# Backward kernel of a speech joint on one core: the last chunk's eight u taken together, with two u on the partitions

## The chip, the cores and the metric

The kernel runs on one core of a Trainium2 chip. The metric is the device time of one execution in microseconds; lower is better. TensorE (PE) multiplies and turns tiles, VectorE (DVE) and ScalarE (ACT) work element by element and empty PSUM, GpSimd (POOL) does small copies and issues a few DMAs, and SyncE (SP) issues nearly all DMAs.

## The reference, cut to what matters

Two strided convolutions with a gelu turn x into f (one row for four rows of x); f and g are mapped by w_f and w_g, added for every pair of a row t and one of eight u, sent through tanh and mapped by w_o. The kernel returns that output and the gradients of all seven inputs.

```python
B, T, D, K = 2, 16000, 256, 3
U = 8
def _fwd_reference(x, w1, w2, g, w_f, w_g, w_o):
    ...
    h = _gelu(h)[:, ::2, :]          # after a convolution of x with w1
    ...
    f = _gelu(f)[:, ::2, :]          # after a convolution of h with w2
    fe = jnp.einsum("btd,de->bte", f, w_f)
    ge = jnp.einsum("bud,de->bue", g, w_g)
    j = jnp.tanh(fe[:, :, None, :] + ge[:, None, :, :])
    return jnp.einsum("btud,dv->btuv", j, w_o)

def reference(x, w1, w2, g, w_f, w_g, w_o, grad_out):
    _out, _vjp = jax.vjp(_f, x, w1, w2, g, w_f, w_g, w_o)
    _grads = _vjp(grad_out)
    return (_out0, *[jnp.asarray(_g) for _g in _grads])
```

All data are bf16; grad_out is [2, 4000, 8, 256].

## The kernel before

The 8000 rows of f (2 batches of 4000) are cut into 17 chunks: one of 256 rows (two blocks of 128), fifteen of 512 (four blocks of 128), and a last one of 64 rows (one block of 64). A chunk g_ goes through three stages:

- `stage_a`: the two convolutions, gelu and its derivative, FE = f by w_f (channels on the partitions), and from the third chunk on `fe_rows`, which turns FE into rows (FER). HR, the rows of h and f, come by a DMA transpose.
- `stage_j`: for each of four pairs of u, `pair(up)` computes JT = tanh(FE + GE) on ACT (L670); JR, the same in rows, from FER + GEB on DVE (L694) and a tanh on ACT (L699); GWO, the gradient of w_o, as JR by GO, the rows of grad_out (one long accumulation in a PSUM bank of its own); for each u the product of GOT (grad_out transposed by DMA) with WOT (w_o turned), which the DVE step L739 multiplies with JSQ - 1 into NGZ while it sums it into NGP (for the gradient of g); the sum over u in ZS, and at the last u in GN (L754); and the output JT by WO, emptied into OUT and stored.
- `stage_de`: from GN back through w_f, w2 and w1: GN (L862), GH (L881, L902), each with a one-column shift (`halo`, on POOL), their rows GNR and GHR (DMA transposes, in the last chunk `pe_rows` on PE, L787), the weight gradients (`wgrad`), and GX, the gradient of x. The w1 gradient of the two last chunks is made at the end by `last_w1`, whose i = 0 part reuses the bank of GWO.

In the last chunk a pair has 64 rows: its GWO matmuls have 64 rows, its output matmuls 64 columns of weights, its GOT matmuls 64 columns of data.

The instructions' order is not written by hand. `op` puts every operation on a list with its engine, an estimated cost, its dependences and a priority (`at`, else `F.now`; in units of rows of f, 512 for a chunk, so one unit is about 0.1 us). `Flow.issue` plays these through with the estimated costs (`c_pe`, `c_act`, `c_dve`, the landing time `land` of a DMA) and gives out, one after another, the operation that could start first, at equal start the one with the lowest priority value. So each engine's order is fixed when the kernel is built. Buffers come in classes with a fixed number of slots (go 4, got 3, jt 3, jr 3, out 3, hr 2, ghr 1, gnr 1, PSUM 7); an operation that opens a buffer waits until a slot is free, and buffers of a class are opened in the order in which they were asked for.

At the start ACT issues the loads of w1 (three), w_f and w_g, with a small gelu between, which brings ACT's table in; POOL issues the loads of g and w_o; SP issues x, w2 and the rest. `turn` transposes weights on PE; w_o's turn gives WOT and has the priority of the middle of chunk 0's convolutions.

Of the kernel before, what the change touches and what calls it, by code (L numbers as in the profile page):

```python
# [188 lines left out]
def c_pe(ns):  # L189
    return sum(max(n / 2.4 + 2.5, 25.0) for n in ns)  # L190
# [20 lines left out]
def kernel(  # L211
# [329 lines left out]
    def stage_a(g_, t0, dt):  # L541
# [60 lines left out]
        if g_ >= NTR:  # L602
            fe_rows(g_)
# [20 lines left out]
    n_gwo = sum(c.nb for c in chunks) * U * KT  # L624
# [29 lines left out]
    def stage_j(g_, t0, dt):  # L654
# [7 lines left out]
        def pair(up):  # L662
# [13 lines left out]
            for h in range(max(nb // 2, 1)):  # L676
# [33 lines left out]
                gwo_ops.append(op("PE", c_pe([V] * (4 * na)), gwo, r=[JR, GO], w=[], at=tu + q * (h / 2 + 0.3)))  # L710
            OUT = buf("out", [P, NB, 2, V], BF16, "OUT_SB")
            for step in range(4):
# [44 lines left out]
                if step < nb:  # L757
                    a = step
                    ps = psum()

                    def out_mm(e, a=a, ps=ps):
                        for jj in range(2):
                            for kt in range(KT):
                                mm(ps[:n_, jj * V:(jj + 1) * V], JT[:, jj, kt, a * n_:(a + 1) * n_], WO[:, kt, :],
                                   kt == 0, kt == KT - 1)
                    op("PE", c_pe([V] * 4), out_mm, r=[JT, WO, (OUT, "b")], w=[ps], new=[ps] + ([OUT] if a == 0 else []))
                    evac(lambda a=a: OUT[:n_, a].rearrange("p u v -> p (u v)"), lambda ps=ps: ps[:n_, :], 512,
                         r=[ps], w=[(OUT, a)])
# [9 lines left out]

    def pe_rows(g_, name, cls, SRC, lo, nblk, m):
        R = buf(cls, [P, 2 * NB + (cls == "ghr"), D], BF16, name)  # L780
# [8 lines left out]
        op("PE", c_pe([P] * (nblk * KT)), trs, r=[SRC, ident], w=[ps], new=[ps, R])  # L789
# [3 lines left out]
    def grad_rows(g_, name, cls, SRC, nblk, m):  # L793
        if chunks[g_].last:
            return pe_rows(g_, name, cls, SRC, 1, nblk, m)
        return tile_rows(g_, name, cls, SRC, nblk, lo=1, shape=[P, 2 * NB + (cls == "ghr"), D],
                         land=3000.0 if g_ == LAST - 1 else 8000.0)
# [265 lines left out]
    def gwg_out():  # L1063
# [10 lines left out]
    CONVS = 4  # L1074
    GEBX = 1.2
# [5 lines left out]
       r=[(warm, 0)], w=[(warm, 1)])  # L1081
# [17 lines left out]
    wload("ACT", WG, 0, lambda: WG[:], lambda: w_g.rearrange("(kt p) n -> p kt n", p=P), BIG, 7000.0)  # L1099
# [5 lines left out]
    wload("POOL", WO, 0, lambda: WO[:], lambda: w_o.rearrange("(kt p) n -> p kt n", p=P), BIG + 2, 9000.0)  # L1105
# [51 lines left out]
    for k in range(NG + 1):  # L1157
        c = chunks[min(k, LAST)]
        t0, Wk = float(c.q0 if k < NG else NQ), float(c.W) if k < NG else 300.0
        if k < NG:  # L1160
            if k in (NTR, CB, CB + 1):
                load_geb(c, lambda up, t0=t0, Wk=Wk, k=k: t0 + Wk * (up / UP - (GEBX if k == NTR else 0.5)))
            for up in range(UP):
# [4 lines left out]
        if k < NG:  # L1168
            stage_j(k, t0, Wk)
# [49 lines left out]
```

## Time and profile before

| what | value |
|---|---|
| median of 3 runs | 782.3 us (781.51 to 782.38) |
| the profiled execution | 781.06 us, span 779.0 us |
| PE busy | 767.7 us (99% of the span), 5641 matmuls |
| DVE, ACT, POOL busy | 718.2, 710.5, 84.0 us |
| granted PE clock | 0.999 |
| last matmul starts / span ends | about 774 / 779.0 us |
| DMA | 183.82 MB, mean 236 GB/s |

Durations in the profile come from the profiled execution; the span is counted from its first to its last record, and the execution's own time is 2.06 us more. A group of matmuls is shown from the first start to the last end; matmuls overlap, so two groups' starts tell more than their busy times. Most matmuls have line 315, the helper `mm`, so they are told apart by their tiles.

### The profile page before, as it was taken

The numbers are of one execution on the slowest core, as the hardware profiler recorded it, in microseconds if no ns is written. First come the engines' busy times: TensorE is split into PE (matmuls) and PEld (weight loads), VectorE is DVE, ScalarE is ACT, GpSimd is POOL, SyncE is SP. The second block draws the span as 40 slices with busy tenths as digits, with TensorE's granted clock in tenths as the row PEclk, the third lists the DMA queues.
The fourth block names the chain that finished last, engine by engine and source line by source line (L and its number), as shares of the span: only waits on it lengthen the run. The fifth ranks groups of instructions, "written<-read, shape, count | busy, mean of one in ns | idle before, by whom it ended". The sixth has DMA issues, their size and how long they took to land.

```text
span 779.0 us, 15414 instructions
## 1 busy us (share of the span) xinstructions
PE 767.7 (99%) x5641; PEld 533.0 (68%) x5641; DVE 718.2 (92%) x1511; ACT 710.5 (91%) x1145; POOL 84.0 (11%) x223
## 2 busy tenths in 40 slices
PE   8999999999999999999999999999999999999997
PEld 6765767576676766767577675766767667677765
DVE  4989999998999999999999999989999899999874
ACT  5989999999999999999999999899999999999752
POOL 2001010101102010020110202001020010201000
PEclk9999999999999999999999999999999999999999
DMA  9999999999999999999999999999999999989783
GB/s 182 228 250 230 230 232 265 250 228 273 205 252 241 240 293 223 280 236 238 257 252 283 204 249 252 236 283 212 272 238 223 254 223 291 191 225 244 187 177 109
DMA packets 393624, 183.82 MB, mean 236 GB/s; under 512 B 318145, under 2 KB 386668, under 8 KB 391628
## 3 DMA queue, kind: packets, MB, share of 16 engines
q1 hardware_dynamic: 391226, 181.64, 102.5%
q10 hardware_dynamic: 2178, 1.05, 0.5%
q8 instruction: 44, 0.72, 0.4%
q0 software_dynamic: 144, 0.15, 0.2%
q14 instruction: 32, 0.26, 0.1%
HBM read 52.99 MB, written 50.35 MB: 133 GB/s over the span
## 4 chain that ended last, share of the span: by engine, by line
PE 89%; ACT 6%; DVE 3%; DMA 2%; issue 1%; ACTq 0%
PE ps L315 74%; PE GWO L315 14%; ACT JT L670 2%; DMA WG<-in_w_g_dram 1%; PE psb L616 1%; ACT JSQ L730 1%; ACT HT L499 1%; ACT g_sq L497 1%; DMA W<-in_w_dram 0%; DVE NGZ L739 0%; ACT JR L699 0%; ACT OUT_SB L324 0%; DVE g_s L501 0%; DVE ZS L754 0%; ACT g_s L509 0%
## 5 line engine op out<-in xcount | busy, mean ns | idle before, releaser
L670 ACT ACTIVATE JT<-FE,GE 128x512 bf16<-128x512 bf16 (+4 forms) x288 | 178.9, 683 | 0.0
L739 DVE SCALAR_TENSOR_TENSOR NGZ<-JSQ,ps 128x512 f32<-128x512 bf16 (+3 forms) x252 | 150.8, 607 | 2.1 <-PE ps L315 1.9
L315 PE MATMUL ps<-WO,JT 128*128 128x256 bf16 (+1 forms) x1008 | 150.5, 273 | 0.3 <-DVE NGZ L739 0.2
L315 PE MATMUL ps<-GOT,WOT 128*128 128x512 bf16 (+2 forms) x544 | 149.9, 362 | 0.3 <-DVE g_s L501 0.3
L730 ACT ACTIVATE JSQ<-JT 128x1024 bf16<-128x1024 bf16 (+2 forms) x129 | 131.0, 1015 | 11.1 <-DVE NGZ L739 8.3
L315 PEld LDWEIGHTS <-JT 128*128 128x128 bf16 (+1 forms) x1008 | 98.3, 98 | 58.3 <-issue 0.4
L324 ACT CAST OUT_SB<-ps 128x512 bf16<-128x512 f32 (+1 forms) x205 | 121.7, 605 | 14.8 <-PE ps L315 14.3
L699 ACT ACTIVATE JR<-JR 128x1024 bf16<-128x1024 bf16 (+1 forms) x116 | 123.5, 1066 | 9.6 <-DVE JR L694 9.6
L315 PE MATMUL GWO<-GO_R,JR 128*128 128x256 bf16 (+1 forms) x1008 | 130.8, 273 | 0.6 <-DVE JR L329 0.6
L754 DVE TENSOR_TENSOR ZS<-ZS,NGZ 128x1024 f32<-128x1024 f32 (+2 forms) x102 | 115.3, 1130 | 0.7
L315 PEld LDWEIGHTS <-JR 128*128 128x128 bf16 (+1 forms) x1008 | 98.2, 98 | 15.8 <-DVE JR L329 0.9
L315 PEld LDWEIGHTS <-W 128*128 128x128 bf16 x636 | 60.0, 98 | 59.8 <-issue 0.7
L315 PE MATMUL ps<-W1T,GH 128*128 128x256 bf16 (+2 forms) x506 | 94.6, 325 | 1.3 <-ACT FE L324 1.2
L315 PE MATMUL ps<-XC,W 128*128 128x512 bf16 (+2 forms) x432 | 86.5, 351 | 0.1
L315 PE MATMUL ps<-GHR,XR 128*128 128x256 bf16 (+1 forms) x736 | 83.3, 273 | 0.0
L315 PEld LDWEIGHTS <-XR 128*128 128x128 bf16 (+1 forms) x756 | 73.7, 98 | 8.6
L694 DVE TENSOR_TENSOR JR<-FER,GEB 128x1024 bf16<-128x1024 bf16 (+1 forms) x116 | 78.0, 673 | 0.0
L315 PEld LDWEIGHTS <-WOT 128*128 128x128 bf16 x544 | 51.0, 98 | 29.6 <-issue 1.9
L819 DVE TENSOR_TENSOR ACC<-ACC,ps 128x512 f32<-128x512 f32 x87 | 57.4, 679 | 14.4 <-PE ps L315 14.3
L315 PEld LDWEIGHTS <-GH 128*128 128x128 bf16 (+1 forms) x506 | 49.4, 98 | 26.3 <-issue 1.9
L326 ACT ACTIVATE GX_SB<-ps 128x512 bf16<-128x512 f32 (+1 forms) x89 | 52.0, 608 | 13.8 <-PE ps L315 13.5
L497 ACT ACTIVATE g_sq<-ps 128x512 bf16<-128x512 f32 (+2 forms) x102 | 57.6, 565 | 2.8 <-PE ps L315 2.8
(131 smaller groups left out, 984.2 us busy)
## 6 DMA issues: line engine op xcount, KB each, us to landing
GO_R<-in_grad_out_dram SPq DMA_DIRECT2D x60, 512.0 KB, 5.2
out_dram<-OUT_SB SPq DMA_DIRECT2D x60, 512.0 KB, 5.5
XR<-in_x_dram SPq DMA_DIRECT2D x15, 1088.0 KB, 8.6
out_dram<-GX_SB SPq DMA_DIRECT2D x30, 512.0 KB, 3.3
GOT<-GO_R SPq DMA_TRANSPOSE x68, 5.3
GO_R<-in_grad_out_dram SPq DMA_DIRECT2D x4, 256.0 KB, 4.1
out_dram<-OUT_SB SPq DMA_DIRECT2D x4, 256.0 KB, 2.6
out_dram<-STAGE SPq DMA_DIRECT2D x6, 128.0 KB, 1.8
```

Of the source, the lines that this page charges most:

```text
L315: nc.tensor.matmul(ps_ap, lhsT=lhsT, rhs=rhs, start=start, stop=stop)
L324: nc.scalar.copy(out=dst(), in_=src())
L326: nc.scalar.activation(out=dst(), in_=src(), func=ACT.Copy, scale=scale)
L497: op("ACT", c_act(W, True), lambda e, mt=mt, ps=ps: nc.scalar.activation(out=sq[:, 0:nb, mt, :n_], in_=blk(ps, c), func=ACT.Square, scale= ...
L499: op("ACT", c_act(W, True), lambda e, mt=mt, ps=ps: nc.scalar.activation(out=h_buf[:, ho:ho + nb, mt, :n_], in_=blk(ps, c), func=ACT.Gelu_ ...
L670: op("ACT", c_act((hi - lo) * nb, ptr=True), lambda e, j=j, mt=mt, lo=lo, hi=hi, b=b: nc.scalar.activation(out=cut(JT[:, j, mt, :W], lo, h ...
L694: op("DVE", c_dve(na * 2 * D, 0.5), lambda e, h=h, na=na, JR=JR: nc.vector.tensor_tensor(out=JR[:n_, 0:na], in0=S["FER"][:n_, 2 * h:2 * h ...
L699: op("ACT", c_act(na * 2 * D), lambda e, na=na, JR=JR: nc.scalar.activation(out=JR[:n_, 0:na], in_=JR[:n_, 0:na], func=ACT.Tanh), r=[JR], ...
L730: nc.scalar.activation(out=JSQ[:, :, :W], in_=JT[:, j, :, :W], func=ACT.Square)
L739: nc.vector.scalar_tensor_tensor(out=cut(Z[:, d2, :W], lo, hi), in0=cut(JSQ[:, d2, :W], lo, hi), scalar=1.0, in1=cut(ps[:, :W], lo, hi), o ...
L754: nc.vector.tensor_tensor(out=o_, in0=i0, in1=i1, op=ALU.add)
L819: op("DVE", c_dve(512), lambda e: nc.vector.tensor_tensor(out=acc_ap().rearrange("p k d -> p (k d)"), in0=acc_ap().rearrange("p k d -> p ( ...
```

## The change

- The last chunk goes through a stage of its own, `stage_j_last`. Row u of JT's 512 columns takes 64 columns, so that one GOT by WOT product covers all eight u, and a block of 128 columns holds two u. grad_out is loaded (`load_last`) with even u on partitions 0 to 63 and odd u on 64 to 127; JR comes from JT by eight transposes on PE instead of from FER, so that GWO takes eight matmuls with 128 rows, and the output eight with 128 columns of weights; the output is stored in two DMAs. The sums over u are a tree on DVE, the sums for the gradient of g two reductions.
- `n_gwo` counts the new number of GWO matmuls, `fe_rows` is left out for the last chunk.
- `DEFER` adds 100 or 130 to the priority values of the GWO and output matmuls of pairs 3 and 2 of the next-to-last chunk; `LATE` adds 100 to those of the last chunk's new stage; `EARLY` is zero.
- The last chunk's GHR takes a slot of the class hr instead of ghr.
- `c_pe` counts at least 45 ns for a matmul, before 25.
- w_o is loaded by ACT behind w_g, before by POOL; the small gelu comes behind all six loads on ACT; w_g's estimated landing is 6500, before 7000.

```diff
--- before.py
+++ after.py
@@ -187,7 +187,7 @@
 def c_pe(ns):
-    return sum(max(n / 2.4 + 2.5, 25.0) for n in ns)
+    return sum(max(n / 2.4 + 2.5, 45.0) for n in ns)
 def c_act(n, psum=False, ptr=False):
@@ -599,7 +599,7 @@
             op("PE", c_pe([c.W] * KT), mms, r=ftk + [WF], w=[ps], new=[ps] + ([FE] if mt == 0 else []))
             evac(lambda mt=mt: FE[:, mt, :c.W], lambda ps=ps: ps[:, :c.W], c.W, r=[ps], w=[(FE, mt)])
         F.now = t0 + 0.55 * dt
-        if g_ >= NTR:
+        if NTR <= g_ < LAST:
             fe_rows(g_)
         F.now = t0 + 0.75 * dt
         tile_rows(g_, "HR", "hr", HT, 3 * nb + 1, shape=[P, 3 * NB + 1, D], land=4500.0)
@@ -621,7 +621,7 @@
-    n_gwo = sum(c.nb for c in chunks) * U * KT
+    n_gwo = sum(c.nb * U for c in chunks[:LAST]) * KT + UP * KT
     gwo_cnt = [0]
     gwo_ops = []
@@ -707,7 +707,7 @@
                                 mm(GWO[:, d2, :], JR[:n_, a, j, d2 * P:(d2 + 1) * P], GO[:n_, 2 * h + a, j, :],
                                    n == 0, n == n_gwo - 1)
                                 gwo_cnt[0] = n + 1
-                gwo_ops.append(op("PE", c_pe([V] * (4 * na)), gwo, r=[JR, GO], w=[], at=tu + q * (h / 2 + 0.3)))
+                gwo_ops.append(op("PE", c_pe([V] * (4 * na)), gwo, r=[JR, GO], w=[], at=tu + q * (h / 2 + 0.3) + DEFER.get((g_, up), 0.0)))
             OUT = buf("out", [P, NB, 2, V], BF16, "OUT_SB")
             for step in range(4):
                 j, d2 = step // 2, step % 2
@@ -763,7 +763,8 @@
                             for kt in range(KT):
                                 mm(ps[:n_, jj * V:(jj + 1) * V], JT[:, jj, kt, a * n_:(a + 1) * n_], WO[:, kt, :],
                                    kt == 0, kt == KT - 1)
-                    op("PE", c_pe([V] * 4), out_mm, r=[JT, WO, (OUT, "b")], w=[ps], new=[ps] + ([OUT] if a == 0 else []))
+                    op("PE", c_pe([V] * 4), out_mm, r=[JT, WO, (OUT, "b")], w=[ps], new=[ps] + ([OUT] if a == 0 else []),
+                       at=F.now + DEFER.get((g_, up), 0.0))
                     evac(lambda a=a: OUT[:n_, a].rearrange("p u v -> p (u v)"), lambda ps=ps: ps[:n_, :], 512,
                          r=[ps], w=[(OUT, a)])
             F.now = tu + q
@@ -776,8 +777,98 @@
+    def load_last(at):
+        c, S = chunks[LAST], st[LAST]
+        n_ = c.np
+        GO = S["GO4"] = buf("go", [P, 2, UP, V], BF16, "GO_R")
+        src = gof[c.q0:c.q0 + n_].rearrange("n (a h) v -> n a h v", h=2)
+        for h in range(2):
+            dma("SP", lambda h=h: GO[h * n_:(h + 1) * n_, 0], lambda h=h: src[:, :, h, :], r=[], w=[(GO, h)],
+                bytes_=n_ * 2048, new=[GO] if h == 0 else [], land=4500.0, load=True, at=at)
+        GOT = S["GOT4"] = buf("got", [P, 2, UP, KT, P], BF16, "GOT")
+        dma("SP", lambda: GOT[:, 0].rearrange("p a k n -> p (a k) n"), lambda: GO[:, 0].rearrange("p a v -> p (a v)"),
+            r=[GO], w=[GOT], bytes_=UP * KT * P * P * 2, new=[GOT], land=4500.0, transpose=True, at=at)
+    def stage_j_last(t0):
+        c, S = chunks[LAST], st[LAST]
+        n_, nb, b, ci = c.np, c.nb, c.bs[0], LAST - CB
+        assert nb == 1 and 2 * n_ == P and U * n_ == CW
+        F.now = t0 + LATE[0]
+        JT = buf("jt", [P, 2, KT, CW], BF16, "JT")
+        GO, GOT = S["GO4"], S["GOT4"]
+        for u in range(U):
+            for mt in range(KT):
+                op("ACT", c_act(n_, ptr=True), lambda e, u=u, mt=mt: nc.scalar.activation(
+                    out=JT[:, 0, mt, u * n_:(u + 1) * n_], in_=S["FE"][:, mt, :n_], func=ACT.Tanh,
+                    bias=GE[:, b, mt, u:u + 1], scale=1.0),
+                   r=[(S["FE"], mt), (GE, b)], w=[(JT, (u, mt))], new=[JT] if u == 0 and mt == 0 else [], at=t0 - 64.0)
+        JR = buf("jr", [P, UP, D], BF16, "JR")
+        tr = psum(BF16)
+        def trs(e):
+            for a in range(UP):
+                for kt in range(KT):
+                    o_ = (a * KT + kt) * P
+                    nc.tensor.transpose(out=tr[:, o_:o_ + P], in_=JT[:, 0, kt, a * P:(a + 1) * P], identity=ident[:])
+        op("PE", c_pe([P] * (UP * KT)), trs, r=[JT, ident], w=[tr], new=[tr, JR])
+        evac(lambda: JR[:].rearrange("p a d -> p (a d)"), lambda: tr[:], UP * D, r=[tr], w=[JR], f=0.5)
+        JSQ = buf("jsq", [P, KT, CW], BF16, "JSQ")
+        op("DVE", c_dve(KT * CW, 0.5), lambda e: nc.vector.tensor_tensor(out=JSQ[:], in0=JT[:, 0], in1=JT[:, 0], op=ALU.mult),
+           r=[JT], w=[JSQ], new=[JSQ])
+        NGZ = buf("ngz", [P, KT, CW], FP32, "NGZ")
+        for d2 in range(KT):
+            ps = psum()
+            def gj(e, d2=d2, ps=ps):
+                for kt in range(KT):
+                    mm(ps[:].rearrange("p (a n) -> p a n", a=UP), WOT[:, kt, d2 * P:(d2 + 1) * P], GOT[:, 0, :, kt, :],
+                       kt == 0, kt == KT - 1)
+            op("PE", c_pe([CW] * KT), gj, r=[GOT, WOT], w=[ps], new=[ps, NGZ] if d2 == 0 else [ps])
+            op("DVE", c_dve(CW), lambda e, d2=d2, ps=ps: nc.vector.scalar_tensor_tensor(
+                out=NGZ[:, d2], in0=JSQ[:, d2], scalar=1.0, in1=ps[:], op0=ALU.subtract, op1=ALU.mult),
+               r=[JSQ, ps], w=[(NGZ, d2)])
+        F.now = t0 + LATE[2]
+        for d2 in range(KT):
+            op("DVE", c_dve(CW), lambda e, d2=d2: nc.vector.tensor_reduce(
+                out=NGP[:, b, d2, :, ci], in_=NGZ[:, d2].rearrange("p (u n) -> p u n", n=n_), axis=mybir.AxisListType.X, op=ALU.add),
+               r=[(NGZ, d2)], w=[(NGP, (b, d2, u, ci)) for u in range(U)])
+        GN = S["GN"] = buf("gn", [P, 2 * NB + 1, KT, P], BF16, "GN")
+        w = CW // 2
+        while w >= n_:
+            last = w == n_
+            op("DVE", c_dve(KT * w), lambda e, w=w, last=last: nc.vector.tensor_tensor(
+                out=GN[:, nb + 1, :, :n_] if last else NGZ[:, :, 0:w], in0=NGZ[:, :, 0:w], in1=NGZ[:, :, w:2 * w], op=ALU.add),
+               r=[NGZ], w=[(GN, "n")] if last else [NGZ], new=[GN] if last else [])
+            w //= 2
+        F.now = t0 + LATE[1]
+        def gwo(e):
+            for a in range(UP):
+                for d2 in range(KT):
+                    n = gwo_cnt[0]
+                    mm(GWO[:, d2, :], JR[:, a, d2 * P:(d2 + 1) * P], GO[:, 0, a, :], n == 0, n == n_gwo - 1)
+                    gwo_cnt[0] = n + 1
+        gwo_ops.append(op("PE", c_pe([V] * (UP * KT)), gwo, r=[JR, GO], w=[]))
+        OUT = buf("out", [P, 2, UP, V], BF16, "OUT_SB")
+        for i in range(UP // 2):
+            ps = psum()
+            def out_mm(e, i=i, ps=ps):
+                for k in range(2):
+                    a = 2 * i + k
+                    for kt in range(KT):
+                        mm(ps[:, k * V:(k + 1) * V], JT[:, 0, kt, a * P:(a + 1) * P], WO[:, kt, :], kt == 0, kt == KT - 1)
+            op("PE", c_pe([V] * 4), out_mm, r=[JT, WO], w=[ps], new=[ps] + ([OUT] if i == 0 else []))
+            evac(lambda i=i: OUT[:, 0, 2 * i:2 * i + 2].rearrange("p a v -> p (a v)"), lambda ps=ps: ps[:], 512,
+                 r=[ps], w=[(OUT, i)])
+        dst_ = outf[c.q0:c.q0 + n_].rearrange("n (a h) v -> n a h v", h=2)
+        for h in range(2):
+            dma("SP", lambda h=h: dst_[:, :, h, :], lambda h=h: OUT[h * n_:(h + 1) * n_, 0], r=[OUT], w=[], bytes_=n_ * 2048)
     def pe_rows(g_, name, cls, SRC, lo, nblk, m):
-        R = buf(cls, [P, 2 * NB + (cls == "ghr"), D], BF16, name)
+        R = buf(cls, [P, 3 * NB + 1 if cls == "hr" else 2 * NB, D], BF16, name)
         st[g_][name] = R
         ps = psum(BF16)
@@ -786,13 +877,13 @@
                 for kt in range(KT):
                     nc.tensor.transpose(out=ps[:m, (a * KT + kt) * P:(a * KT + kt + 1) * P],
                                         in_=SRC[:, lo + a, kt, :m], identity=ident[:])
-        op("PE", c_pe([P] * (nblk * KT)), trs, r=[SRC, ident], w=[ps], new=[ps, R])
+        op("PE", c_pe([P] * (nblk * KT)), trs, r=[SRC, ident], w=[ps], new=[ps, R], at=F.now - EARLY)
         evac(lambda: R[:m, 0:nblk].rearrange("p a d -> p (a d)"), lambda: ps[:m, 0:nblk * D], nblk * D, r=[ps], w=[R], f=0.5)
         return R
     def grad_rows(g_, name, cls, SRC, nblk, m):
         if chunks[g_].last:
-            return pe_rows(g_, name, cls, SRC, 1, nblk, m)
+            return pe_rows(g_, name, "hr" if cls == "ghr" else cls, SRC, 1, nblk, m)
         return tile_rows(g_, name, cls, SRC, nblk, lo=1, shape=[P, 2 * NB + (cls == "ghr"), D],
                          land=3000.0 if g_ == LAST - 1 else 8000.0)
@@ -1072,13 +1163,17 @@
     BIG = -1e9
     CONVS = 4
+    LEAD = 0.3
+    LATE = (100.0, 100.0, 100.0)
+    DEFER = {(LAST - 1, 3): 100.0, (LAST - 1, 2): 130.0}
+    EARLY = 0.0
     GEBX = 1.2
     F.now = BIG
     warm = buf("gsq", [P, KT, CW], BF16, "g_sq")
     op("DVE", 200.0, lambda e: nc.vector.memset(warm[:, 0, 0:2 * P], 0.0), w=[(warm, 0)], new=[warm])
     op("ACT", 1400.0, lambda e: nc.scalar.activation(out=warm[:, 1, 0:8], in_=warm[:, 0, 0:8], func=ACT.Gelu_apprx_tanh),
-       r=[(warm, 0)], w=[(warm, 1)])
+       r=[(warm, 0)], w=[(warm, 1)], at=BIG + 5.0)
     wps = psum()
     WARM = 20
@@ -1096,13 +1191,13 @@
     for i in range(KK):
         wload("ACT", W1, i, lambda i=i: W1[:, i], lambda i=i: w1[i].rearrange("(kt p) n -> p kt n", p=P), BIG, 4000.0)
     wload("ACT", WF, 0, lambda: WF[:], lambda: w_f.rearrange("(kt p) n -> p kt n", p=P), BIG, 6500.0)
-    wload("ACT", WG, 0, lambda: WG[:], lambda: w_g.rearrange("(kt p) n -> p kt n", p=P), BIG, 7000.0)
+    wload("ACT", WG, 0, lambda: WG[:], lambda: w_g.rearrange("(kt p) n -> p kt n", p=P), BIG, 6500.0)
+    wload("ACT", WO, 0, lambda: WO[:], lambda: w_o.rearrange("(kt p) n -> p kt n", p=P), BIG, 7000.0)
     for b in range(B):
         dma("POOL", lambda b=b: GR8[:, b, :], lambda b=b: g[b], r=[], w=[(GR8, b)], bytes_=4096, at=BIG + 1, land=6000.0)
     load_xc(1, BIG, 60.0)
     dma("SP", lambda: W2[:].rearrange("p i k n -> p (i k) n"), lambda: w2.rearrange("i (kt p) n -> p (i kt) n", p=P),
         r=[], w=[(W2, i) for i in range(KK)], bytes_=393216, load=True, at=BIG - 1.0, land=2500.0, behind=[xl_ops[-1]])
-    wload("POOL", WO, 0, lambda: WO[:], lambda: w_o.rearrange("(kt p) n -> p kt n", p=P), BIG + 2, 9000.0)
     def turn(jobs, at, behind=()):
@@ -1160,13 +1255,15 @@
         if k < NG:
             if k in (NTR, CB, CB + 1):
                 load_geb(c, lambda up, t0=t0, Wk=Wk, k=k: t0 + Wk * (up / UP - (GEBX if k == NTR else 0.5)))
-            for up in range(UP):
+            if k == LAST:
+                load_last(t0 - CW * LEAD)
+            for up in range(UP if k < LAST else 0):
                 load_go(k, up, t0 + Wk * (up // 2 * 2 / UP - 0.6), [got_op[0, up - 2]] if k == 0 and up > 1 else ())
                 load_got(k, up, t0 + Wk * (up / UP - 0.6))
         if 0 < k < LAST:
             load_xc(k + 1, t0 - Wk * 0.3)
         if k < NG:
-            stage_j(k, t0, Wk)
+            stage_j(k, t0, Wk) if k < LAST else stage_j_last(t0)
         if k + 1 < NG:
             stage_a(k + 1, t0, Wk)
         if k >= 1:
```

## The prediction

> **What bounds the kernel now.** I read the page first, then the chain of waits over the last 60 us, then the timeline of each engine at the end and at the start, then the waits of PE.
>
> ```profile
> PE 767.7 (99%) x5641; PEld 533.0 (68%) x5641; DVE 718.2 (92%) x1511; ACT 710.5 (91%) x1145; POOL 84.0 (11%) x223
> ...
> PE 89%; ACT 6%; DVE 3%; DMA 2%; issue 1%; ACTq 0%
> ...
> 100.00:720.00 620.00, 619.73 (x4441) 426.24 (x4440) 592.25 (x1188) 590.89 (x920) 66.99 (x168) 1.00 1.07 245
> 743.50:774.60 31.10, 31.07 (x264) 21.39 (x262) 20.54 (x75) 14.47 (x35) 2.04 (x10) 1.00 0.58 132
> ```
>
> The first two lines are the page's busy times and its chain by engine. The others are stretches: length, then busy time of PE, PEld, DVE, ACT and POOL, clock, DMA share, GB/s. PE is idle for 0.27 us of the 620 us in the middle and for 0.03 us of the 31.1 us in which the last chunk is worked off (743.5 to 774.6), at full clock. A microsecond of PE work taken out there is a microsecond of the end, as long as something else stands ready for PE. The 4.4 us behind the last matmul (an eviction of GX, its store, the close) are not touched.
>
> How dear the half-filled last chunk is, the PE timeline shows (start, busy, tile, shape, count):
>
> ```profile
> 742.87 0.59 PE L315 MATMUL ps<-GOT,WOT 128*128 128x512 bf16 x2
> 743.30 0.60 PE L315 MATMUL ps<-WO,JT 128*128 128x256 bf16 x4
> 743.74 1.04 PE L315 MATMUL GWO<-GO_R,JR 128*128 128x256 bf16 x8
> 744.61 0.22 PE L315 MATMUL ps<-GOT,WOT 128*128 128x64 bf16 x2
> 744.76 0.62 PE L315 MATMUL ps<-WO,JT 128*64 128x256 bf16 x4
> 745.32 0.23 PE L315 MATMUL ps<-GOT,WOT 128*128 128x64 bf16 x2
> 745.48 0.61 PE L315 MATMUL GWO<-GO_R,JR 64*128 64x256 bf16 x4
> 746.02 0.29 PE L315 MATMUL ps<-GOT,WOT 128*128 128x64 bf16 x4
> ```
>
> Busy times overlap, so a group costs from its start to the next start. Whole groups of the chunk before: 0.43 us for two 512-wide, 0.44 for four 256-wide, 0.87 for eight GWO: 0.109 us per 256 columns. The half ones: four out matmuls 745.32 - 744.76 = 0.56, four GWO matmuls 746.02 - 745.48 = 0.54. They are not cheaper for having 64 rows or columns; they cost 0.1 more per group.
>
> **The change part by part. (1) The last chunk's matmuls.** Each sum is over the groups in the PE timeline from 744 to 763, start to next start.
> - GWO: four groups of 0.54 = 2.16 us become 8 full matmuls, 0.87. Gain 1.29.
> - Out: four groups of 0.56 = 2.24 become 8 full ones, 0.87. Gain 1.37.
> - GOT by WOT: 32 matmuls of 64 columns stand in twelve groups that take 1.74 us together (54 ns each); they become four of 512, two times 0.43. Gain 0.87.
> - The two transposes of FE (726.96 to 727.19, 0.23) go. Eight transposes of JT come; eight of L688 took 35.89 to 36.33, 0.44. Loss 0.21.
>
> Sum: 3.32 us less PE work, nearly all of it in the stretch without PE idle.
>
> For the 64-column matmuls the Trainium skill has another price: "TensorE: Matmul & The Clock Gate", Back-to-back issue gap, gives N/2.4 + 2.5 ns when warm, and its part on the 56 ns gap a floor of about 25 ns; by that the 32 cost some 0.94 us, their merging gains 0.07, and the sum is 2.5 instead of 3.3. The trace measures 54 ns each (1.74 us), so the row is taken.
>
> **(2) ACT and DVE of that chunk** are beside PE (14.5 and 20.5 of 31.1 us busy). Off: four JR tanh (0.63 each), four adds (0.41), eight JSQ (0.3), sixteen NGZ steps (0.22 with 0.08 for the accumulator), eight adds to ZS or GN (0.29), two of four evictions. On: one JSQ of 1024 (0.6 at most), two NGZ of 512 (0.67 each), two reductions of 512, a tree of 512, 256 and 128 elements (0.68, about 0.5, 0.29). For a reduction of 512 no row exists; between the reduction of 144 elements (0.30) and 512-wide fp32 work (0.69), I take 0.69. As one chain JSQ to GN is 0.6 + 1.34 + 1.38 + 1.47 = 4.8 us on DVE, where the pairs took about 1.5 us each in between PE work. It costs nothing only while PE has other work; rival D prices that.
>
> **(3) Order.** Out and GWO matmuls of the next-to-last chunk's pairs 2 and 3 (3.5 us each pair) get later priorities, the last chunk's J stage comes behind the next-to-last chunk's D/E stage, and GHR of the last chunk takes a slot of "hr", so that it no longer waits until all of last_w1's first halves have read the one "ghr" slot. The same matmuls are done; order can only make or close gaps, and there is 0.03 us to close. The 45 ns floor in c_pe moves only order: it touches matmuls of up to 102 columns, which the last chunk alone has in number. New idle: bounds 0 and 1 us, taken 0.2, near the 0.27 that the same planner leaves in 620 us.
>
> **(4) SP's queue.** Four 64 KB loads and four transposes become two loads of 128 KB and one transpose; four stores become two. On SP a load's issue takes 0.51 and a transpose of such a piece 1.2 to 1.5, so 3 to 4 us of SP time fall away, off the path; the load stands 154 columns (15 us) ahead and landed in 2.3 us, its transpose in 2.3.
>
> **(5) The start.** w_o leaves POOL's queue and becomes ACT's sixth load, ahead of the table.
>
> ```profile
> 0.74 3.43 DMA W<-in_w_dram
> 4.17 0.02 issue
> 4.19 9.90 DMA WG<-in_w_g_dram
> ...
> PE ps L315 <- DMA WG<-in_w_g_dram: 1.6, 1, 1.6
> ...
> 1.24 1.28 ACT L1080 ACT_TABLE_LOAD   x1 [1.24 <-PEq L1203]
> ...
> q10 hardware_dynamic: 1360, 0.66, 6.4%
> q0 software_dynamic: 144, 0.15, 3.6%
> ```
>
> These are the chain's first pieces, PE's waits to 60 us, ACT's table load in its timeline, and the queues in the first 45 us (packets, MB, share of 16 engines). WG, ACT's fifth load, was issued only when the first had landed at 4.17. If the sixth waits likewise for the second, it goes out near 5.4 (estimate, one 1.2 us step on); behind it now stand the table load (1.28) and the warm ACTIVATE (0.21), so ACT is free near 7.3. Its next work, the first copy of XC (6.40 in its timeline), starts 0.9 late, but the second copy (7.74), behind which the convolution starts, has that slack: cost 0 to 0.2.
>
> PE waits 1.6 us for WG, landed at 14.1, and conv2 (14.74) stands behind it. POOL's queue used 3.6% x 16 x 45 / 0.15 = 173 engine-us per MB, ACT's 6.4% x 16 x 45 / 0.66 = 70. Moving 0.13 MB frees 13.5 engine-us, 0.85 us of 16 busy engines, ahead of WG. But w_o now lands behind WG, and its turn into WOT moves ahead on PE: the planner has it at 2725 + 341 + 7000 = 10.1 us instead of 2810 + 341 + 9000 = 12.2, just as the first convolutions end, so conv2 may wait for it. WG at 13.2, w_o 0.6 later (its share on ACT's queue), then WOT's, WF's and WG's work (0.23 + 0.23 + 0.6) puts conv2 at 14.85: a loss of 0.1. Bounds: a gain of 1.6 if both land before PE asks, a loss of 1.9 if w_o follows WG by the 2.8 us that fit the slowest landing here. I take the loss of 0.1.
>
> The Trainium skill speaks against a gain here: "DMA: Bandwidth & Descriptors", Issuing engines are not separate DMA queues, says that all issuers share the same 16 engines and that another issuer saves only issue time. By it the 0.85 is nothing and the sum 2.2 instead of 3.0; the rows show queues of unequal engine time per byte, so they are used.
>
> **Sum.** 781.06 (profiled execution; span 779.0 and 2.06 around it) - 3.32 + 0.2 + 0.1 = 778.0. The median of the runs is 782.3, 1.24 above the profiled one, so the forecast is 779.3.
>
> **The rivals.** A is the forecast, 779.3, give or take 1 for idle and order.
>
> B: w_g and w_o both land before PE is done with the first convolutions. For: the freed engine time. Against: WG trailed its issue by 9.9 us. The wait of 1.6 goes as well as the 0.1: 777.6.
>
> C: w_o lands last and PE stands at its turn, 1.9 late instead of 0.1: 781.1, within the noise.
>
> D, the slower side: the last chunk's chain is left bare. Its J stage has lower priority than the next-to-last chunk's work. If PE has used up its fill before the GOT matmuls of the last chunk run, it waits for DVE's NGZ, reductions and tree (4.2 us) and then for the D/E steps between its small matmuls (L862 0.33, POOL's shift 0.3, L881/L902 0.5, again 0.3, GHR's copy 0.6, with hand-overs 2.2). The fill: last_w1 of the next-to-last chunk (three times 1.84), the last chunk's GWO and out (1.74) and the g gradients (1.26), 8.5 us in all against 6.4 of waits. It decides from the point where over 2.1 us of that fill runs ahead; all of it ahead costs 6.4 - 3.3 = 3.1: 785.4. Against: the planner starts what can start first, last_w1 has the lowest priority but GX, and it waits for a DMA transpose of GHR (issue 752.7, matmuls from 763).
>
> E: it doesn't do what it says for time: gaps of some 3 us open where the matmuls went, 782.3. Against: 0.03 us of idle there now.
>
> **How the numbers follow.** About 0.2% (1.6 us) is what a measurement of this kernel can tell from no change. A 0.57, B 0.15, C 0.12, D 0.10, E 0.06. A and B are faster by over 0.2% (under 780.7); of C a third is; E, most of C and a fifth of D are within. Faster 0.76, same 0.15, slower 0.09. The range runs from B less 0.6 (777.0) past C to the first part of D (782.6); out of it fall the rest of D and B's far end.
>
> **What would show it.** Right: GWO and out of the last chunk in 8 full matmuls of 0.109 us, 4 GOT matmuls of 512, PE idle from 740 to its last matmul under 0.5 us, PE busy about 764.4. PE's wait for WG shows at the start, perhaps renamed WO. Wrong: PE idle of over 2 us behind NGZ, GN or GH near the end (D, E), or a wait for WO past 15 us (C).

## The result, and the profile after

The changed kernel takes 775.58 us (median of 4 runs, 774.49 to 776.05) against 782.34 (781.51 to 782.71): ratio 0.9914, with a 95% interval of 0.9901 to 0.9928, or 6.8 us less. The forecast was 779.3, from 777.0 to 782.6: the direction was right, the size less than half of what came, and the result lies below the range. The profiled execution took 775.74 us, its span 773.9.

PE's busy time and the chain by engine come from the page; the stretches have the columns length, PE, PEld, DVE, ACT, POOL, clock, DMA share, GB/s.

```profile
PE 764.1 (99%) x5603; PEld 531.7 (69%) x5603; DVE 718.6 (93%) x1480; ACT 704.6 (91%) x1127; POOL 82.5 (11%) x222
...
PE 86%; ACT 6%; DVE 5%; issue 1%; DVEq 0%; ACTq 0%
```

```profile
740.00:750.00 10.00, 10.00 (x76) 6.81 (x74) 8.60 (x15) 3.28 (x6) 1.40 (x7) 1.00 0.69 172
750.00:760.00 10.00, 10.00 (x83) 7.11 (x80) 6.19 (x14) 5.50 (x11) 0.46 (x3) 1.00 0.47 137
760.00:770.00 10.00, 9.80 (x95) 7.95 (x93) 5.29 (x14) 1.80 (x4) 0.30 (x1) 1.00 0.53 149
```

PE is busy for 764.1 us (forecast about 764.4), without a gap over the last 30 us; the 0.20 us missing in the last stretch lie behind the last matmul, at 769.8. The 2% of DMA have gone from the chain. On PE's timeline (start, busy, tile, shape, count) the last chunk's new work is short, and fits the prices of the full groups of before:

```profile
744.14 0.61 PE L814 MATMUL psb<-ident,JT 128*128 128x128 bf16 x8
744.59 2.75 PE L315 MATMUL ps<-GN,W2T 128*128 128x512 bf16 x12
747.18 1.03 PE L315 MATMUL ps<-GOT,WOT 128*128 128x512 bf16 x4
748.04 1.04 PE L315 MATMUL GWO<-GO_R,JR 128*128 128x256 bf16 x8
748.91 3.41 PE L315 MATMUL ps<-W1T,GH 128*128 128x512 bf16 x20
...
758.25 1.04 PE L315 MATMUL ps<-WO,JT 128*128 128x256 bf16 x8
759.22 0.61 PE L315 MATMUL ps<-NGR,GR 8*128 8x256 bf16 x4
```

From start to next start: transposes 0.45, GOT 0.86, GWO 0.87. The eight out matmuls stand 0.97 before the next group.

To see where the 6.8 us went I set three marks in PE's timeline: the first matmul of the third chunk's convolution, that of the next-to-last chunk's, and the end of the last matmul.

| us | before | after | difference |
|---|---|---|---|
| third chunk's first convolution | 51.39 | 50.00 | -1.39 |
| from there to the next-to-last chunk's | 606.92 | 606.82 | -0.10 |
| from there to the end of the last matmul | 116.26 | 112.98 | -3.28 |
| behind the last matmul | 4.4 | 4.1 | -0.3 |

The tail gives what was forecast for it. The start, forecast as a loss of 0.1, gives 1.4 in this pair of profiles and 2.5 on the mean over all profiles (below). Its trace after the change shows why there is no wait for w_g or w_o any more; first what was issued, by ACT, SP and PE:

```profile
2.80 0.56 ACTq L341 DMA_DIRECT2D WG<-in_w_g_dram  x1
4.28 0.41 ACTq L341 DMA_DIRECT2D WO<-in_w_o_dram  x1
...
3.99 7.16 SPq L339 DMA_TRANSPOSE XC<-in_x_dram  x2
...
11.66 0.40 PE L1211 MATMUL psb<-ident,WO 128*128 128x128 bf16 x4
...
12.56 0.35 PE L315 MATMUL ps<-gT,WG 128*128 128x8 bf16 x8
...
13.31 1.47 PE L315 MATMUL ps<-HT,W 128*128 128x256 bf16 x12
```

In the kernel before the same queues stood so:

```profile
4.19 0.37 ACTq L341 DMA_DIRECT2D WG<-in_w_g_dram  x1
...
2.15 11.65 SPq L339 DMA_TRANSPOSE XC<-in_x_dram  x2
...
14.14 0.36 PE L315 MATMUL ps<-gT,WG 128*128 128x8 bf16 x8 [1.56 <-DMA WG<-in_w_g_dram]
```

w_g now goes out at 2.80 instead of 4.19 and lands 6.1 us later (8.9) instead of 9.9 (14.1); w_o goes out at 4.28 and lands 6.3 later (10.6). Both are there before PE asks at 11.66. And SP's two transposes of x, issued at 2.15 before, go out at 3.99 and hold SP for 7.16 us instead of 11.65. The loads' order changed through a count that no line of the diff shows: in the kernels' instruction lists the loads of SP and ACT take eight completion semaphores in turn, so the ninth waits for the first. (The traces show the waits as late issues, not the semaphores.) Before, w_g was ninth, behind the first transpose; with the gelu moved back, ACT gives out its loads sooner, w_g is eighth, w_o ninth (it goes out once the first w1 load has landed) and the transpose tenth.

### The profile page after: what moved, and what is told of

It is laid out like the page before. It is cut to its first block, busy times and chain, and to the rows that moved or that the text cites. A ratio compares the mean times of both kernels' runs of the same rounds, so it can differ in the third digit from the quotient of the medians.

```text
span 773.9 us, 15268 instructions
## 1 busy us (share of the span) xinstructions
PE 764.1 (99%) x5603; PEld 531.7 (69%) x5603; DVE 718.6 (93%) x1480; ACT 704.6 (91%) x1127; POOL 82.5 (11%) x222
## 4 chain that ended last, share of the span: by engine, by line
PE 86%; ACT 6%; DVE 5%; issue 1%; DVEq 0%; ACTq 0%
PE ps L315 72%; PE GWO L315 13%; ACT JT L670 2%; ACT JSQ L730 1%; PE psb L616 1%; ACT HT L499 1%; ACT g_sq L497 1%; DVE NGZ L739 1%; DVE g_s L501 1%; ACT JR L699 1%; DVE G L501 0%; ACT OUT_SB L324 0%; DVE ZS L754 0%; ACT g_s L509 0%; DVE g_sq L513 0%
## 5 line engine op out<-in xcount | busy, mean ns | idle before, releaser
L670 ACT ACTIVATE JT<-FE,GE 128x512 bf16<-128x512 bf16 (+3 forms) x272 | 174.4, 700 | 0.0
L315 PE MATMUL ps<-WO,JT 128*128 128x256 bf16 x1000 | 148.7, 273 | 0.3 <-DVE NGZ L739 0.2
L739 DVE SCALAR_TENSOR_TENSOR NGZ<-JSQ,ps 128x512 f32<-128x512 bf16 (+2 forms) x238 | 148.2, 631 | 0.1
L315 PE MATMUL ps<-GOT,WOT 128*128 128x512 bf16 (+1 forms) x516 | 147.9, 372 | 0.3 <-DVE g_s L501 0.3
L730 ACT ACTIVATE JSQ<-JT 128x1024 bf16<-128x1024 bf16 (+1 forms) x122 | 128.9, 1057 | 8.8 <-DVE NGZ L739 6.2
L324 ACT CAST OUT_SB<-ps 128x512 bf16<-128x512 f32 x203 | 120.5, 605 | 15.3 <-PE ps L315 15.0
L315 PE MATMUL GWO<-GO_R,JR 128*128 128x256 bf16 x1000 | 129.4, 273 | 0.6 <-DVE JR L329 0.6
L699 ACT ACTIVATE JR<-JR 128x1024 bf16<-128x1024 bf16 x112 | 120.9, 1081 | 9.0 <-DVE JR L694 9.0
L754 DVE TENSOR_TENSOR ZS<-ZS,NGZ 128x1024 f32<-128x1024 f32 (+1 forms) x96 | 113.5, 1182 | 0.6
L315 PEld LDWEIGHTS <-JR 128*128 128x128 bf16 x1000 | 97.7, 98 | 16.0 <-DVE JR L329 0.9
```

What stands on the lines that cost most here:

```text
L315: nc.tensor.matmul(ps_ap, lhsT=lhsT, rhs=rhs, start=start, stop=stop)
L324: nc.scalar.copy(out=dst(), in_=src())
L670: op("ACT", c_act((hi - lo) * nb, ptr=True), lambda e, j=j, mt=mt, lo=lo, hi=hi, b=b: nc.scalar.activation(out=cut(JT[:, j, mt, :W], lo, h ...
L699: op("ACT", c_act(na * 2 * D), lambda e, na=na, JR=JR: nc.scalar.activation(out=JR[:n_, 0:na], in_=JR[:n_, 0:na], func=ACT.Tanh), r=[JR], ...
L730: nc.scalar.activation(out=JSQ[:, :, :W], in_=JT[:, j, :, :W], func=ACT.Square)
L739: nc.vector.scalar_tensor_tensor(out=cut(Z[:, d2, :W], lo, hi), in0=cut(JSQ[:, d2, :W], lo, hi), scalar=1.0, in1=cut(ps[:, :W], lo, hi), o ...
```

## The experiments

### The start: four ways

Two causes were in dispute: the place of w_g (before or behind the transposes) and the queue of w_o (POOL's or ACT's). The first run is the whole start without the rest, the others split it.

Start only, the rest as before:

```diff
 # the kernel before
-       r=[(warm, 0)], w=[(warm, 1)])
+       r=[(warm, 0)], w=[(warm, 1)], at=BIG + 5.0)
-    wload("ACT", WG, ..., BIG, 7000.0)
+    wload("ACT", WG, ..., BIG, 6500.0)
+    wload("ACT", WO, ..., BIG, 7000.0)
-    wload("POOL", WO, ..., BIG + 2, 9000.0)
```

> The kernel before with the start's edits alone (w_o on ACT, the small gelu behind all six loads, w_g's landing 6500). The changed kernel's second convolution starts at 13.31 us instead of 14.74 and its third chunk's first convolution at 50.00 instead of 51.39, 1.39 earlier, and it keeps 1.4 to 1.5 up to 656.8. If the start is a term of its own: second convolution at 13.3, 50.0 for the third chunk, span 779.0 - 1.5 = 777.5, median near 780.8. If the start's gain needs the new tail's plan too: less than half of it, over 781.6.

Only the small gelu moved behind the loads; w_o stays on POOL:

```diff
 # the kernel before
-       r=[(warm, 0)], w=[(warm, 1)])
+       r=[(warm, 0)], w=[(warm, 1)], at=BIG + 5.0)
```

> The kernel before with one edit: the small gelu stands behind ACT's loads; w_o stays with POOL. Then w_g is issued without a wait and the first transpose of chunk 1's x behind it waits for the first w1 load. Order theory (w_g was late because chunk 1's transposes were issued at 2.15, ahead of it at 4.19): w_g issued near 2.8, landed under 10, the wait of PE gone, second convolution near 13.3, span near 777.5. Queue theory (POOL's queue for w_o took the engines' time): w_o still moves there while w_g does, so w_g lands after 12, PE waits for it, second convolution after 14.

Only w_o moved to ACT; the gelu stays in front:

```diff
 # the kernel before
-    wload("ACT", WG, ..., BIG, 7000.0)
+    wload("ACT", WG, ..., BIG, 6500.0)
+    wload("ACT", WO, ..., BIG, 7000.0)
-    wload("POOL", WO, ..., BIG + 2, 9000.0)
```

> The kernel before with w_o on ACT behind w_g (landing 6500), the small gelu still first, so that the first transpose of chunk 1's x is issued at 2.15 ahead of w_g, which waits for the first w1 load. Order theory: w_g lands near 13 to 14 and w_o behind it, PE stands at w_o's turn, second convolution at 14.7 to 16.5, span 779 to 781. Queue theory: 0.85 us of engine time are free, w_g lands near 13 or before, second convolution under 14, span under 778.3.

The whole change, but w_g and w_o held behind the first transpose of chunk 1's x:

```diff
 # the kernel after; xc_ops is a new list of load_xc's transposes
-    wload("ACT", WG, ..., BIG, 6500.0)
-    wload("ACT", WO, ..., BIG, 7000.0)
...
     load_xc(1, BIG, 60.0)
+    wload("ACT", WG, ..., BIG, 6500.0, behind=[xc_ops[0]])
+    wload("ACT", WO, ..., BIG, 7000.0, behind=[xc_ops[0]])
```

> The changed kernel with w_g and w_o issued behind the first transpose of chunk 1's x (the small gelu then stands ahead of the two on ACT). Order theory: the start's gain is gone, second convolution at 14.7 to 16.5 instead of 13.31, span 773.9 + 1.4 to 3.2 = 775.3 to 777.1. Queue theory: w_o is not on POOL's queue, so the gain stays, second convolution near 13.3, span near 773.9.

Measured (the kernel before has 782.15 beside them; the two last columns are from the profile of each):

| kernel | median us | ratio, 95% | w_g out, landed | second convolution |
|---|---|---|---|---|
| start only | 779.41 | 0.9961 (0.9946 to 0.9975) | 2.79, 8.4 | 12.93 |
| gelu only | 779.43 | 0.9960 (0.9945 to 0.9975) | 2.81, 8.7 | 12.50 |
| w_o only | 779.51 | 0.9966 (0.9953 to 0.9978) | 4.21, 11.2 | 12.53 |
| all, w_g behind | 775.83 | 0.9923 (0.9903 to 0.9942) | 3.93, 11.1 | 12.44 |

Gelu only (the timeline with issues by ACT and SP and the second convolution; then the queue of POOL in the first 16 us: packets, MB, share of 16 engines):

```profile
2.81 0.49 ACTq L341 DMA_DIRECT2D WG<-in_w_g_dram  x1
...
4.12 6.80 SPq L339 DMA_TRANSPOSE XC<-in_x_dram  x2
...
12.50 1.47 PE L315 MATMUL ps<-HT,W 128*128 128x256 bf16 x12
```

```profile
q0 software_dynamic: 112, 0.14, 2.9%
```

w_o only:

```profile
4.21 0.37 ACTq L341 DMA_DIRECT2D WG<-in_w_g_dram  x1
4.63 0.90 ACTq L341 DMA_DIRECT2D WO<-in_w_o_dram  x1
...
2.16 9.18 SPq L339 DMA_TRANSPOSE XC<-in_x_dram  x2
...
12.53 1.48 PE L315 MATMUL ps<-HT,W 128*128 128x256 bf16 x12
```

Either cause alone was refuted: gelu only speaks against the queue theory, the other two against the order theory. With w_o still on POOL's queue the wait for w_g is gone once w_g stands ahead of the transposes; with w_g behind the transposes it is gone once w_o has left POOL's queue. W_o only leaves a little: PE stands idle for 0.42 us ahead of w_o's turn, whose weight load waits 0.6 us for w_o to land. The gains don't add, since there is only one wait to remove. It needs both: the transposes ahead of w_g, and w_o among them by way of POOL.

That also tells what POOL's queue cost. Its line in the first 16 us of the kernel before reads:

```profile
q0 software_dynamic: 112, 0.14, 9.8%
```

The same 112 packets took 9.8% of the engines' time there (6.5 to 8.0% in the three other profiles with the old start) and 2.9% in gelu only. So the time per byte was not the queue's own: it is stretched by what it runs beside. On this the Trainium skill ("DMA: Bandwidth & Descriptors", Issuing engines are not separate DMA queues) says that all issuers run on the same 16 engines and that another issuer saves only issue time. For the price per byte gelu only bears that out. W_o only is 2.6 us faster than before, but it does not contradict the rule: with the issuer the time of issue changed too, from 2.72 us (POOL) to 4.63 us, behind w_g.

What was not separated: whether POOL's queue does the harm or only w_o's early issue, and whether w_o delays the transposes or they delay it. SP's issue of the two transposes took 11.65 us (before), 9.18 (w_o only), 6.80 (gelu only), so both changes shorten it.

### The tail: four ways

The new last chunk with the start of before:

```diff
 # the kernel after: the start's edits taken back
-       r=[(warm, 0)], w=[(warm, 1)], at=BIG + 5.0)
+       r=[(warm, 0)], w=[(warm, 1)])
-    wload("ACT", WG, ..., BIG, 6500.0)
-    wload("ACT", WO, ..., BIG, 7000.0)
+    wload("ACT", WG, ..., BIG, 7000.0)
+    wload("POOL", WO, ..., BIG + 2, 9000.0)
```

> The changed kernel with the start as before (small gelu first, w_o on POOL, w_g's landing 7000). If the two parts add: second convolution back at 14.7, third chunk at 51.4, and from the first convolution of the next-to-last chunk to the end of the last matmul 112.98 us as in the changed kernel (before: 116.26); median about 782.2 minus 3.6 = 778.6. If the tail's gain hangs on the start's plan: less than 2 us.

The order that the priorities had before:

```diff
 # the kernel after
-    LATE = (100.0, 100.0, 100.0)
-    DEFER = {(LAST - 1, 3): 100.0, (LAST - 1, 2): 130.0}
+    LATE = (0.0, 0.0, 0.0)
+    DEFER = {}
```

> The changed kernel without DEFER and with LATE at zero, so that the next-to-last chunk's output and GWO matmuls come at once and the last chunk's new stage at its old place. Theory (the end is worth only the PE time taken out, order nothing): 112.98 us from the next-to-last chunk's first convolution to the end of the last matmul, within 0.3, PE idle under 0.3 in it, time as the changed kernel's, 775.6. Rival (the deferred work covers the last chunk's chain): PE idle of 1 us or more near the end, over 776.6.

GHR of the last chunk back in the one slot of its class:

```diff
 # the kernel after, pe_rows and grad_rows
-        R = buf(cls, [P, 3 * NB + 1 if cls == "hr" else 2 * NB, D], BF16, name)
+        R = buf(cls, [P, 2 * NB + (cls == "ghr"), D], BF16, name)
-            return pe_rows(g_, name, "hr" if cls == "ghr" else cls, SRC, 1, nblk, m)
+            return pe_rows(g_, name, cls, SRC, 1, nblk, m)
```

> The changed kernel with the last chunk's GHR back in the class ghr. Theory: the same PE work, 112.98 within 0.3; but GHR's transposes now come almost last, so that turn, copy on ACT (0.6) and its 12 matmuls stand at the end: PE idle of 0.6 to 1.0 us there at most. Rival: no difference at all.

Both of these, and the floor in `c_pe` back at 25:

```diff
 # the kernel after, with the two diffs above, and
-    return sum(max(n / 2.4 + 2.5, 45.0) for n in ns)
+    return sum(max(n / 2.4 + 2.5, 25.0) for n in ns)
```

> The changed kernel with all edits of order undone (no DEFER, LATE zero, ghr, 25 ns in c_pe): the new stage and the start alone. Theory: 113.0 to 114.0 (that of GHR's slot), 775.6 to 776.6. Rival (without the order edits gaps open where the matmuls went): 115 or more, over 777.6.

Measured (beside 782.43 of the kernel before). The segment is the one from the next-to-last chunk's first convolution to the end of the last matmul, 116.26 before and 112.98 after:

| kernel | median us | ratio, 95% | segment | against after |
|---|---|---|---|---|
| tail only | 778.14 | 0.9939 (0.9916 to 0.9962) | 112.69 | -0.29 |
| no DEFER, LATE | 776.65 | 0.9925 (0.9903 to 0.9948) | 114.61 | +1.63 |
| GHR in its own slot | 775.85 | 0.9914 (0.9892 to 0.9935) | 113.85 | +0.87 |
| none of the order | 777.36 | 0.9934 (0.9910 to 0.9958) | 115.30 | +2.32 |

The medians of the three order runs stand 0.3 to 1.8 us above the changed kernel's 775.58, in the same order as their segments, but the intervals overlap; the verdict rests on the segments, one profile each, and on what PE waits for. The 0.29 by which tail only is shorter is not explained. From 700 to 764 us, no DEFER and LATE first, then the changed kernel:

```profile
700.00:764.00 64.00, 62.78 (x513) 45.04 (x512) 52.09 (x121) 45.52 (x93) 7.24 (x21) 1.00 0.81 199
```

```profile
700.00:764.00 64.00, 63.96 (x528) 46.55 (x527) 55.40 (x127) 44.82 (x91) 7.06 (x21) 1.00 0.78 200
```

PE is idle for 1.22 us without the priorities and 0.04 with them. Its waits from 700 to 780 us (engine, line, what for: us, times, longest) name DVE's GN there (L953, which was L862 before):

```profile
PE ps L315 <- DVE GN L953: 1.2, 2, 0.8
```

Whose GN it is, the timelines show. PE's longer wait of the two stands ahead of products of 512 columns, so this is the GN of the next-to-last chunk; the last chunk's has 64. On DVE (second view) its two steps come behind the last chunk's new NGZ steps and reductions:

```profile
748.45 2.60 PE L315 MATMUL ps<-GN,W2T 128*128 128x512 bf16 x11 [0.82 <-DVE GN L953]
```

```profile
744.10 1.28 DVE L829 SCALAR_TENSOR_TENSOR NGZ<-JSQ,ps 128x512 f32<-128x512 bf16 x2
745.30 1.28 DVE L834 TENSOR_REDUCE NGP<-NGZ 128x8 f32<-128x512 f32 x2
746.51 0.69 DVE L953 SCALAR_TENSOR_TENSOR GN<-G,ps 128x512 bf16<-128x512 bf16 x1
747.11 0.68 DVE L841 TENSOR_TENSOR NGZ<-NGZ 128x512 f32<-128x512 f32 x1
747.72 0.68 DVE L953 SCALAR_TENSOR_TENSOR GN<-G,ps 128x512 bf16<-128x512 bf16 x1
```

In the changed kernel GN comes first, and PE has a deferred group of GWO and the eight transposes to do meanwhile (743.27 to 744.59):

```profile
743.21 1.27 DVE L953 SCALAR_TENSOR_TENSOR GN<-G,ps 128x512 bf16<-128x512 bf16 x2
...
747.98 1.28 DVE L829 SCALAR_TENSOR_TENSOR NGZ<-JSQ,ps 128x512 f32<-128x512 bf16 x2
```

Which of the two helps more, LATE on DVE or DEFER on PE, was not separated. With GHR in its own slot PE waits for ACT's copy of it, just ahead of the last w1 matmuls:

```profile
767.93 0.60 PE L315 MATMUL GWO<-GHR,XR 65*128 65x256 bf16 x4 [0.72 <-ACT GHR L324]
```

So the new stage does open waits of PE when nothing is done about order: with none of it the segment is 0.96 shorter than before instead of 3.28. Of the 3.3 us taken off PE, 2.3 would have come back, 1.9 of them as the two waits shown (1.2 and 0.7 in that run too); the rest is in no wait that the view lists. What the floor of 45 ns does by itself was not tried: the two other edits add up to 2.50, more than the 2.32 of all three, so nothing is left over for it that these profiles could show.

### What the profiled executions hide

Two more runs of the kernel before and one of the kernel after, a single execution each, were made to see how much its waits vary; beside them, a version of the changed kernel that counts on GNR and GHR landing later:

```diff
 # the kernel after
-                         land=3000.0 if g_ == LAST - 1 else 8000.0)
+                         land=3000.0 if g_ == LAST - 1 else 10000.0)
```

> The kernel before once more, for a second profile of the same program. From the first convolution of the first chunk to that of the third takes 43.01 us in its first profile, 41.48 in six of the seven profiles without PE's wait for w_g, and 45.24 in the changed kernel with the old start. Theory (the wait for w_g differs from execution to execution, and the first profile has a short one): 43 to 46 here, the excess over 41.48 equal to the wait that PE shows for w_g within 0.2. Rival (the profile is typical and the medians' larger gain comes from elsewhere): 43.0 within 0.2.

> As the run before: a third profile of the kernel before. Theory: 43 to 46 us from the first convolution of the first chunk to that of the third, with an excess over 41.48 that equals the wait for w_g; the mean excess of the three profiles over 2 us. Rival: 43.0 within 0.2 again.

> The changed kernel once more. Theory: its start has no such wait, so 41.48 us within 0.1 again, and 112.98 within 0.3 from the next-to-last chunk's first convolution to the end of the last matmul; what differs from its first profile lies in the first convolution's start (7.2 to 8.5) and in waits for GNR's DMA transpose in the middle (0 to 2.2).

> The changed kernel with 10000 instead of 8000 for the estimated landing of GNR's and GHR's DMA transposes, so that the weight gradients stand later in PE's order. In four profiles PE waited 0.6 to 2.2 us in the middle for GNR's transpose, in the others not. If these waits are the bulk of what differs between executions and the new order opens no others: no wait for GNR in the profile, median 0.3 to 1.0 under the changed kernel's 775.6. If the plan is upset instead (SP's order changes too): equal or slower.

Measured: before 784.38 and 780.29, after 775.09; the later landing 775.04 (774.60 to 775.55, ratio 0.9905, 0.9889 to 0.9920, beside 783.19). PE's waits of the first repeat of the kernel before, then of the second:

```profile
PE ps L315 <- DMA GNR<-GN: 1.9, 1, 1.9
PE psb L1116 <- DMA WF<-in_w_f_dram: 1.6, 1, 1.6
...
PE ps L315 <- DMA WG<-in_w_g_dram: 0.7, 1, 0.7
```

```profile
PE ps L315 <- DMA WG<-in_w_g_dram: 1.3, 1, 1.3
```

The old start costs a different amount each time. The profiles with it wait 1.56 (before), 1.3 (second repeat) and 2.3 us (tail only) for w_g, and the first repeat 2.9 us for weights: w_f, w_g and, for 0.6, w1. From the first convolution to the third chunk these four take 42.8 to 45.8 us. The seven profiles with the whole new start, gelu only and the one with w_g held behind all take 41.47 or 41.48; w_o only takes 42.24. So the changed kernel's repeat came out as expected, and so did the second repeat of the kernel before (an excess of 1.28 for a wait of 1.3).

In the two others the wait is not all. The first repeat exceeds 41.48 by 4.35 us with 2.9 us of waits, tail only by 3.76 with 2.3: 1.45 us are left over in both. There the granted clock of TensorE fell at the end of the waits. From 14.0 to 17.5 us (columns as above), the first repeat and then the first profile of the same kernel:

```profile
14.00:17.50 3.50, 3.15 (x22) 2.02 (x22) 1.36 (x6) 1.42 (x5) 0.00 (x0) 0.51 1.02 263
```

```profile
14.00:17.50 3.50, 3.36 (x43) 2.57 (x44) 2.33 (x9) 1.90 (x6) 0.02 (x1) 1.00 0.97 255
```

The 12 matmuls of the second convolution take 2.57 us there instead of 1.48. Tail only has a clock of 0.52 from 14.5 to 18.0 us. With the waits of 1.3 and 1.56 us the clock stayed at 1.00, and no other profile has such a stretch ahead of its last matmul. Time and mean clock are on record for 29 more executions of the kernel before, most of them without a trace: 23 have a clock of 0.998 or less and take 783.0 us on the mean, 6 have 0.999 or more and take 780.9. The first profile, 781.06 at 0.999, goes with the six. That the 23 had the same stretch at half clock is likely but not shown.

What still varies in all profiles is when the first convolution begins, from 6.95 to 8.52 us.

On the means, the four profiles with the old start (before, its two repeats, tail only) reach the third chunk at 51.84 us and the seven with the new one (after, its repeat, start only, the three order runs, the later landing) at 49.30. Of these 2.5 us some 2.0 are waits for weights and 0.7 the two stretches at half clock (1.45 in two of four profiles), less 0.2 because the first convolution happened to begin earlier in the four.

A second thing varies, in the middle: in some profiles PE waited for the DMA transpose of GNR, 1.9 us in the first repeat of the kernel before, 0.6 in tail only, 1.2 in gelu only, 2.2 in w_o only. No profile with the whole new start shows it. Nothing in the change touches that transpose in the middle chunks, so this may be chance. The later landing was tried to find out; but its profile and the changed kernel's two show no such wait alike, and its median is level with the changed kernel's single run beside it (775.04 and 775.09). By the letter it did what was expected, no wait and 0.5 us under 775.6, but so did the changed kernel itself, so the cause stays open.

## Why the prediction was right or wrong

**Step (1), PE's work: right.** Forecast 3.32 off, measured 3.28 in the segment. The row of 54 ns for a 64-column matmul was the one to take. The price set against it, from the Trainium skill's "TensorE: Matmul & The Clock Gate" (Back-to-back issue gap), is an estimate of 29 ns for 64 columns by the formula there, and makes the sum 2.5; the same section warns that this formula under-counts small matmuls that each load their weights, and the 54 ns agree with the warning.

**Step (2), ACT and DVE: right with the order given.** No wait of PE is left in the changed kernel's last 70 us.

**Step (3), order: the number right, the reason wrong.** 0.2 of new idle was taken; 0.04 from 700 to 764 us came. But the step says that the same matmuls are done and that order has only 0.03 us to close. That is counted on the old work. The new stage brings new gaps, which the order then closes: 2.3 us of them, by the last run of the tail. Rival D saw the danger but not the way it comes. It has PE wait for the last chunk's own chain, NGZ to GN; what came without the order was a wait of 1.2 us for the next-to-last chunk's GN, behind the last chunk's new steps on DVE. Of D's list only GHR's copy showed, at 0.7 us. DEFER and LATE and the other slot are what keeps both away.

**Behind the last matmul: not in the sum.** It was said that the 4.4 us are not touched; they became 4.1. The last store, of the w1 gradient, is issued as long after the last matmul as before (1.06 and 1.03 us), but lands 1.9 us after its issue instead of 2.4. GX's two stores now go out earlier ahead of it, since four w1 matmuls stand behind the last GX matmuls; whether that is the reason no run shows.

**Step (5), the start: wrong, and the largest part of the miss.** The value taken was a loss of 0.1 between bounds of -1.6 and +1.9 (by its own terms the upper one is 2.3: w_o at 16.0 and 1.06 of turns and products put the second convolution at 17.06); -1.4 came in the first pair of profiles, the outcome of rival B, whose 777.6 was given 0.15. Two terms failed. "WG at 13.2" kept w_g's issue at 4.19 and moved only the engine time of POOL's queue: I saw that w_g was issued as the first load landed, called it the fifth of ACT, and let the sixth wait for the second. The count runs over SP's and ACT's loads together, so moving the gelu put w_g 1.4 us earlier and ahead of the transposes. And 173 engine-us per MB for POOL's queue was read as its own price; 2.9% instead of 9.8% for the same packets shows that it was crowding. The turn of w_o, which was to hold the second convolution at 14.85, found w_o landed 1.1 us before (10.6 against 11.66).

**The step "Sum": wrong.** It carried the 1.24 us between the profiled execution and the median over as a constant. The changed kernel's median is 0.16 below its profiled execution, so 1.4 of the 3.7 us by which the forecast missed lie here, and 1.5 in step (5). Part of the 1.24 was the old start, which goes: its wait cost 1.56 in the profiled execution and up to 2.9 in others, and in two of the four profiles the clock fell with it, for 1.45 more.

**The whole.** On the means over the profiles the start gives 2.5, the tail 3.28, the part behind the last matmul 0.3 and the absent GNR waits 0.6 (mean over the four old-start profiles), 6.7 in all for 6.76 measured. The parts measured alone agree: start only 2.74 and tail only 4.29 give 7.03. The 0.6 for GNR is an observed difference without a shown cause.

## What to carry to other kernels

When work is taken from an engine that is never idle, ask what the engines beside it will now do, and in which order: here 2.3 of 3.3 us would have come back without a new order, among other things because DVE did the last chunk's steps ahead of the ones that PE needed next, although the profile before had no gap to show for it. A wait for one DMA at the start is a race between all the transfers under way, so look up which load each load waits for before it is issued, and take a second and a third profile before its length is used in a sum. Look at the granted clock around the wait as well: the wait and what a lower clock costs are two terms.

## What the runs showed of the hardware

- Plain weight loads among the DMA transposes of x land late: w_g 9.9 us after its issue behind them with w_o on POOL (before), 7.0 and 7.2 behind them without (w_o only, w_g behind), 5.0 to 6.1 in the profiles that have it ahead of them.
- The issue of those two transposes holds SP for 11.0 to 11.9 us when they go ahead of w_g with w_o on POOL (four profiles), 9.1 and 9.2 ahead of w_g with w_o on ACT, 6.4 to 7.3 behind w_g.
- In the two profiles with PE's longest waits for weights at the start (2.9 us in three pieces, and 2.3 in one) the granted clock was about 0.5 for some 3.4 us, from 14.0 and 14.6 us on, and twelve matmuls took 2.57 us instead of 1.48; in the two with waits of 1.3 and 1.56 us it stayed at 1.00.
- Two executions of the kernel before on one chip differed by 4.1 us (784.38 and 780.29): 2.1 up to the third chunk, by waits for weights of 2.9 and 1.3 and the stretch at half clock, less 1.0 for an earlier first convolution, and 2.0 in the middle, where one waited 1.9 for GNR.
